# Causal attention with a decaying bias, followed by a GELU feed-forward, on one core: other loads of the first k, chunk 0 by pairs of subtiles, v of batch 2 behind the x tiles

## The chip, the core and the metric

The kernel runs on one core of a Trainium2 chip. The time is the device time of one execution in microseconds (us); the figure to compare is the median over several runs. TensorE does the matrix products, VectorE and ScalarE the element-wise work, GpSimd and SyncE mostly issue DMAs. In the profile they are called PE, DVE, ACT, POOL and SP; PEld is TensorE's loading of weights, and SPq is SyncE's queue of DMA issues.

## The reference

q, k and v have the shape (8 batches, 8 heads, 576 positions, 64), s has (8, 8, 576). The feed-forward has 512 inputs, 2048 hidden units and 512 outputs, all in fp32.

```
scores = scale * np.matmul(q, k.transpose(0, 1, 3, 2))
cum = np.cumsum(np.maximum(s, 0.0), axis=-1)
bias = -(cum[:, :, :, None] - cum[:, :, None, :])
scores = np.where(causal, -1000000000.0, scores + np.minimum(bias, 0.0))
attn = softmax(scores)                       # max subtracted, exp, divided by the sum
x = np.matmul(attn, v), laid out as (8 * 576 tokens, 8 * 64)
out = gelu_exact(x @ w_in) @ w_out
```

## The kernel before, in words

**How the bias is handled.** The bias is a difference of a term of the row and a term of the column. The row's term cancels in the softmax, so `weights` (L217) forms exp(cum) for each position, `scale_v` (L202, on VectorE) multiplies v by it, and `den_col` (L212) puts it into a 65th column of v, which gives the sum. At the end a certificate (`cert_decay` L239, `cert_1` to `cert_4`) proves from the largest q, k (`absmax` L188, VectorE) and v (`square_v` L194, ScalarE) that this shortcut was exact enough; otherwise a slow path runs, which these inputs don't take.

**Loads.** `load_qk` (L85) brings q (i = 0) or k (i = 1) of one batch and one group of four heads in four DMAs of 32 partitions, from GpSimd's queue, which turns fp32 into bf16 on the way. `load_v` (L109) brings v of a batch in five DMAs as fp32, from the queue it is given. `load_w` (L130) brings a quarter of w_in (which = 0) or of w_out (which = 1), again cast by GpSimd's queue. A buffer called rawv (L106) exists twice, so v of batch b + 2 waits until v of batch b has been read.

**Attention of a batch.** `tr_qk` (L180) transposes 32 x 32 blocks of q or k on VectorE. `sc_item` (L329) multiplies k and q for a group g and a half u of the blocks below the diagonal, and takes the exp on ScalarE; `sc_first` (L353) does this for batch 0 and adds the mask on TensorE. `mk_item` (L340) masks the diagonal blocks on VectorE. `av_item` (L403) multiplies with v for a group and a row tile `it` of 128 positions, and divides by the sum on VectorE (L418, L419). When both groups of a row tile are there, `to_xT` (L383) transposes it, by a DMA on SyncE's queue (L388), or on TensorE with a copy by VectorE (L392, L395).

**Feed-forward.** The 4608 tokens are taken in nine chunks of 512, which straddle the batches. `l1_item` (L430) computes 256 hidden units of a chunk on TensorE (L441) and their gelu on ScalarE (L446). `l2_item` (L450) sums over a range of the 16 hidden tiles for given subtiles of 128 tokens (L457), copies each finished subtile out of its output buffer (L465 by ScalarE in chunk 0, L467 by VectorE in the others), and stores it. The output buffers have the tag mlp, and there are two of them.

**Order.** Every engine executes its instructions in the order in which the program lists them; that order is written by hand. In the main loop (L532) chunk c runs layer 1, with late attention items of batch c and the transposes, scaling and squares of batch b = c + 1 between its eight items. Then it runs layer 2 in four subtiles of four slots each (`groups`, L477). After slot i the items in `side[i]` follow, the attention of batch c + 1. Chunk 0 has its own lists (`late` L539 and `side` L578). Exp and gelu are in different tables of ScalarE: `exp_set` (L471) and `gelu_set` (L474) load them. `filler` (L397) issues matmuls on zeros.

On GpSimd's queue the order after the start is: v of batch 0 (two pieces), w_in 0, v (three pieces), w_in 1 to 3, then for each group two quarters of w_out and q and k of batch 1, then v of batch 1, then q and k of batch 2 (L490 to L500, L597). On SyncE's queue v of batch 2 is issued ahead of the fourth subtile of chunk 0 (L591).

Of the kernel before, what the change touches and what calls it, by code (L numbers as in the profile page):

```python
# [19 lines left out]
def kernel(  # L20
# [10 lines left out]
    nc = tc.nc  # L31
    fp32 = mybir.dt.float32
# [52 lines left out]
    def load_qk(b, i, g):  # L85

        if (b, "qk") not in raws:
            raws[b, "qk"] = work.tile([128, 2, HG, S * 2], bf16, tag="rawqk", bufs=2, name="raw_qk")
        src = q if i == 0 else k
        for h in range(4):  # L90
            nc.gpsimd.dma_start(  # L91
                out=raws[b, "qk"][h * 32 : h * 32 + 32, i, g, :].rearrange("p (t c) -> p t c", c=2 * D),
                in_=bass.AP(
                    tensor=src.tensor,
                    offset=src.offset + (b * H + 4 * g + h) * S * D,
                    ap=[[2 * D, 32], [64 * D, SB], [1, 2 * D]],
                ),
            )

    def load_qks(b):  # L100
        for g in range(HG):
            for i in range(2):
                load_qk(b, i, g)
# [5 lines left out]
    def load_v(b, eng, sts=range(ST)):  # L109
        t = raws[b, "v"] if (b, "v") in raws else raw_v(b)  # L110
        for st in sts:
# [7 lines left out]
                ),  # L119
            )  # L120

    s_sw = const.tile([64, S], fp32, name="s_sw")
    nc.sync.dma_start(out=s_sw, in_=s.flatten_outer_dims())
    load_qk(0, 0, 0)
    load_qk(0, 1, 0)

    w_in_r = const.tile([128, KO, dff], bf16, name="w_in_r")
    w_out_r = const.tile([128, FT, KO * 128], bf16, name="w_out_r")
# [19 lines left out]
        channel_multiplier=1,  # L148
    )
    load_qk(0, 0, 1)  # L150
    load_qk(0, 1, 1)
    amx = const.tile([128, B * HG, 2], fp32, name="amx")
    wb = const.tile([128, ST, BH], bf16, name="wb")
    xT = const.tile([128, NP, n_tok], bf16, name="xT")
# [81 lines left out]
    def le(dst, a, thr, op=ALU.is_le):  # L236
        nc.vector.tensor_scalar(dst, a, float(thr), None, op0=op)

    def cert_decay():  # L239

        w64 = work.tile([64, S], fp32, tag="w64", bufs=1, name="w64")
        nc.scalar.activation(w64, cum, func=AF.Exp)
        W = const.tile([64, ST], fp32, name="cW")
        nc.vector.tensor_reduce(
            W[:, 0 : ST - 1], w64[:, 0:512].rearrange("p (s c) -> p s c", c=128), axis=AX, op=ALU.add
        )
        nc.vector.tensor_reduce(W[:, ST - 1 : ST], w64[:, 512:S], axis=AX, op=ALU.add)

        le(goods[:, 0:1], cum[:, 0:1], -MAX_C, ALU.is_ge)
        le(goods[:, 1:2], cum[:, 511:512], 2.0, ALU.is_ge)  # L250
        le(goods[:, 2:3], cum[:, S - 1 : S], MAX_C)
        le(goods[:, 3:4], cum[:, 255:256], -14.0, ALU.is_ge)

        nc.vector.tensor_copy(drop[:, 0:1], W[:, 0:1])
        nc.vector.tensor_tensor(drop[:, 1:2], drop[:, 0:1], W[:, 1:2], op=ALU.add)
        nc.vector.tensor_tensor(drop[:, 2:3], drop[:, 1:2], W[:, 2:3], op=ALU.add)
        le(goods[:, 4:5], drop[:, 1:2], 2.0)
        nc.vector.tensor_tensor(keep[:, 0:1], drop[:, 2:3], W[:, 3:4], op=ALU.add)
        le(goods[:, 5:6], keep[:, 0:1], math.exp(66.0))

        nc.vector.tensor_scalar(keep, W[:, 1:4], EPS, None, op0=MULT)
# [135 lines left out]
    def filler(n):  # L397

        f_ps = ps.tile([128, NB], fp32, tag="mlp", bufs=2, name="f_ps")
        for _ in range(n):  # L400
            nc.tensor.matmul(f_ps, lhsT=zero[:, :128], rhs=zero, start=True, stop=True)  # L401
# [69 lines left out]
    def exp_set():  # L471
        nc.scalar.preload_act_table_set("natural_log_exp_and_others")
# [11 lines left out]


    exp_set()
    filler(16)
    weights()
    filler(5)
    load_v(0, nc.gpsimd, range(2))  # L490
    load_w(0, 0)
    load_v(0, nc.gpsimd, range(2, ST))
    for i in range(1, 4):
        load_w(0, i)
    for g in range(HG):
        load_w(1, 2 * g)
        load_w(1, 2 * g + 1)
        for i in range(2):
            load_qk(1, i, g)
    load_v(1, nc.gpsimd)  # L500
    tr_qk(0, 0, 0)
    masks()
# [3 lines left out]
    den_col(0)  # L506
    tr_qk(0, 0, 1)
    tr_qk(0, 1, 1)
    filler(4)
    for st in range(2):  # L510
        scale_v(0, st)
    sc_first(1, 0)
    av_item(0, 0, 0)
    av_item(0, 0, 1)
    sc_first(1, 1)
# [3 lines left out]
    to_xT(0, 0, True)  # L519
    filler(1)  # L520
    to_xT(0, 1, True)
    for st in range(2, ST):
        scale_v(0, st)
    gelu_set()

    sc, mk, av = sc_item, mk_item, av_item
# [5 lines left out]
    for c in range(NCH):  # L532
        b = c + 1
        if c > 0 and b + 1 < B:
            load_qks(b + 1)
            load_v(b + 1, nc.sync)
        if c == 0:

            late = [  # L539
                [(av, 0, 0, 2)], [(av, 0, 1, 2)], [(av, 0, 0, 3)], [(av, 0, 1, 3), (to_xT, 0, 2, True)],  # L540
                [(av, 0, 0, 4)], [(av, 0, 1, 4), (to_xT, 0, 3, True)], [], [(to_xT, 0, 4, True)],
            ]
            for half in range(2):
                for f2 in range(FT // 2):
                    l1_item(0, f2, half * 256, half * 256 + 256)
                    for f, *a in late[f2] if half == 0 else []:
                        f(*a)
                    if half == 1 and 1 <= f2 <= ST:
                        square_v(0, f2 - 1)
            for g in range(HG):  # L550
                absmax(0, g)
        else:
            for f2 in range(FT // 2):
                l1_item(c, f2)
                for g, it in late_of.get(c, [])[f2 : f2 + 1]:
                    av(c, g, it)
                if b < B and f2 < HG:
                    tr_qk(b, 0, f2)
                    tr_qk(b, 1, f2)
                if b < B and f2 == 2:  # L560
                    den_col(b)
                    for st in range(2):
                        scale_v(b, st)
                if b < B and f2 == 3:
                    for st in range(2, ST):
                        scale_v(b, st)
                if b < B and 4 <= f2 < 4 + HG:
                    absmax(b, f2 - 4)
                if b < B and 1 <= f2 <= ST:
                    square_v(b, f2 - 1)  # L570
        if b < B:
            if c == 0:
                for i in range(2):
                    tr_qk(b, i, 0)
                den_col(b)
            exp_set()
            if c == 0:
                side = [[] for _ in range(16)]  # L578
                side[2] = [(sc, b, 0, 0)]
                side[5] = [(sc, b, 0, 1), (mk, b, 0, 0), (tr_qk, b, 0, 1), (tr_qk, b, 1, 1)]  # L580
                side[7] = [(scale_v, b, 0), (scale_v, b, 1), (mk, b, 0, 1)]
                side[8] = [(sc, b, 1, 0), (av, b, 0, 0), (scale_v, b, 2)]
                side[9] = [(av, b, 0, 1), (scale_v, b, 3)]
                side[10] = [(av, b, 0, 2), (mk, b, 1, 0), (scale_v, b, 4)]
                side[11] = [(sc, b, 1, 1), (av, b, 0, 3), (av, b, 1, 0)]
                side[12] = [(av, b, 1, 1), (mk, b, 1, 1)]
                side[14] = [(av, b, 1, 2, True), (av, b, 1, 3, True)]
                side[15] = [(to_xT, b, 2, True), (to_xT, b, 3, True)]
                for sub in range(4):
                    if sub == 3:  # L590
                        load_v(2, nc.sync)  # L591
                    groups(c, (sub,), side[4 * sub : 4 * sub + 4])
                for st in range(ST):
                    square_v(b, st)
                cert_decay()
                gelu_set()
                load_qks(2)  # L597
                for g in range(HG):
                    absmax(b, g)
            else:  # L600

                side = [[] for _ in range(16)]
                sc_at = (2, 5, 7, 10) if b < 4 else (2, 5, 8, 11)
                for at, (g, u) in zip(sc_at, [(0, 0), (1, 0), (0, 1), (1, 1)]):
                    side[at].append((sc, b, g, u))
                side[sc_at[3]].append((gelu_set,))
                for at, (g, u) in zip((5, 8, 11, 13 if b < 4 else 14), [(0, 0), (1, 0), (0, 1), (1, 1)]):
                    side[at].append((mk, b, g, u))
                for at, (g, it) in zip((6, 7, 9, 10), [(0, 0), (0, 1), (1, 0), (1, 1)]):
                    side[at].append((av, b, g, it))  # L610
                if b < 4:
                    side[12].append((av, b, 0, 2))
                    side[13].append((av, b, 1, 2, True))
                    side[14].append((to_xT, b, 2, True))
                for sub in range(4):
                    groups(c, (sub,), side[4 * sub : 4 * sub + 4])
        else:
            for sub in range(4):
                l2_item(c, (sub,))
                if c == B - 1:  # L620
                    (cert_1, cert_2, cert_3, cert_4)[sub]()
# [150 lines left out]
```

## Time and profile before

| | |
|---|---|
| median of 5 runs | 337.67 us (335.5 to 338.04) |
| profiled execution | 339.84 us |
| its span, first to last instruction | 338.1 us |
| mean granted clock of TensorE | 0.976 |
| PE busy | 315.5 us (93%) |
| DVE, ACT, POOL busy | 190.2, 185.1, 92.1 us |
| layer 1 of chunk 0 | from 24.50 us |
| layer 2 of chunk 0 | from 41.23 us |
| layer 1 of chunk 1 | from 73.72 us |
| layer 1 of chunk 2 | from 110.26 us |
| read from, written to memory | 36.85 MB, 9.44 MB |

The profile is of one execution. Times within it count from its first instruction. A line of the chain of waits or of the timeline has the start, the duration, the engine, the line of the program, the operation and the tiles written and read; in brackets stands how long the engine was idle before, and what ended that. "x4" is the number of instructions put together. A line of the waits view has the engine and line that waited, what it waited for, the total, the number of times and the longest. The clock row gives tenths of the full clock in 40 slices of the span, where 9 stands for nine tenths or more.

### The profile page before, as it was taken

The page shows a single profiled execution, that of the slowest core. Times are in us where ns is not written, and L with a number is a line of the kernel's source. Part 1 is how long each engine was busy: PE and PEld are TensorE (multiplying, and loading weights), DVE is VectorE, ACT ScalarE, POOL GpSimd, SP SyncE. Part 2 cuts the span into 40 slices and gives each one's busy share as a digit, 9 for nine tenths or more (in the row PEclk, how much of TensorE's full clock was granted, in tenths as well). Part 3 has the DMA queues.
Part 4 walks back from the last instruction along what each step waited for, and adds up shares of the span by engine and source line. Part 5 has one row for each costly group of instructions (what it writes and reads, how often), then busy time and mean ns, then how long its engine had stood idle before and what let it go on. Part 6 is the DMA issues. An engine that isn't in the chain of part 4 may idle for free.

```text
span 338.1 us, 6339 instructions
## 1 busy us (share of the span) xinstructions
PE 315.5 (93%) x2554; PEld 157.3 (47%) x2554; DVE 190.2 (56%) x393; ACT 185.1 (55%) x247; POOL 92.1 (27%) x152
## 2 busy tenths in 40 slices
PE   8999969729998999899999999999999999999992
PEld 3358824414444544454455444545454545444440
DVE  7355815777746783679358845965695542150020
ACT  2464855545864586558567755776587464205400
POOL 8962657608490009000910190000000000000000
PEclk9999989967999999999999999999999999999998
DMA  8999999999794709670997198901310221110011
GB/s 90 147 231 202 116 160 237 163 233 168 67 149 109 183 14 137 129 181 17 120 146 186 27 149 138 182 8 64 93 33 8 80 80 31 41 62 32 3 66 67
DMA packets 92373, 36.76 MB, mean 109 GB/s; under 512 B 82992, under 2 KB 87088, under 8 KB 92336
## 3 DMA queue, kind: packets, MB, share of 16 engines
q0 software_dynamic: 43872, 16.00, 39.8%
q1 hardware_dynamic: 48464, 20.28, 23.6%
q8 instruction: 22, 0.36, 0.5%
q14 instruction: 15, 0.12, 0.1%
HBM read 36.85 MB, written 9.44 MB: 137 GB/s over the span
## 4 chain that ended last, share of the span: by engine, by line
PE 75%; DMA 14%; POOL 6%; DVE 2%; issue 1%; ACT 1%; POOLq 0%
PE h_ps L441 34%; PE o_ps L457 32%; DMA w_out_r<-in_moe_w_out_dram 7%; POOL raw_qk L91 5%; PE av L409 4%; PE sc_ps L321 4%; DMA w_in_r<-in_moe_w_in_dram 2%; DMA raw_v<-in_v_dram 2%; POOL raw_v L113 1%; DMA raw_qk<-in_k_dram 1%; DMA xT<-x 1%; DVE P L344 1%; DVE o_sb L467 1%; ACT sq L197 0%; DVE x L419 0%
## 5 line engine op out<-in xcount | busy, mean ns | idle before, releaser
L441 PE MATMUL h_ps<-xT,w_in_r 128*128 128x512 bf16 (+1 forms) x640 | 135.4, 363 | 8.4 <-DMA xT<-x 7.7
L457 PE MATMUL o_ps<-w_out_r,gT 128*128 128x512 bf16 x576 | 136.7, 382 | 2.8 <-DMA w_out_r<-in_moe_w_out_dram 2.8
L446 ACT ACTIVATE gT<-h_ps 128x1024 bf16<-128x1024 f32 (+1 forms) x80 | 75.0, 939 | 76.8 <-PE h_ps L441 76.1
L441 PEld LDWEIGHTS <-w_in_r 128*128 128x128 bf16 x640 | 60.1, 99 | 64.0 <-DMA xT<-x 7.8
L457 PEld LDWEIGHTS <-gT 128*128 128x128 bf16 x576 | 52.3, 98 | 60.7 <-issue 7.0
L336 ACT ACTIVATE P<-sc_ps 128x1024 bf16<-128x1024 f32 x56 | 54.3, 1021 | 37.1 <-PE sc_ps L321 37.1
L91 POOL DMA_DIRECT2D raw_qk<-in_q_dram x64 | 38.7, 621 | 94.0 <-DVE amx L189 89.6
L467 DVE COPY o_sb<-o_ps 128x512 f32<-128x512 f32 x32 | 22.1, 692 | 63.8 <-PE o_ps L457 63.8
L91 POOL DMA_DIRECT2D raw_qk<-in_k_dram x64 | 38.8, 626 | 14.0 <-DMA w_out_r<-in_moe_w_out_dram 7.8
L189 DVE TENSOR_REDUCE amx<-raw_qk 128x2 f32<-128x2304 bf16 x16 | 40.2, 2536 | 0.0
L418 DVE RECIPROCAL rc<-av 128x4 f32<-128x4 f32 (+1 forms) x80 | 14.3, 179 | 42.9 <-PE av L409 42.8
L409 PEld LDWEIGHTS <-P 128*128 128x128 bf16 x576 | 27.4, 98 | 19.7 <-DVE P L344 3.4
L419 DVE TENSOR_TENSOR x<-av,rc 128x256 bf16<-128x256 f32 (+1 forms) x80 | 33.8, 423 | 2.8
L409 PE MATMUL av<-vv,P 128*128 128x65 bf16 x576 | 31.3, 194 | 2.4 <-DVE P L344 2.0
L205 DVE TENSOR_TENSOR vv<-raw_v,wb 128x512 bf16<-128x512 f32 (+1 forms) x40 | 25.9, 690 | 5.6 <-DMA raw_v<-in_v_dram 5.6
L182 DVE STREAM_TRANSPOSE qkT<-raw_qk 128x576 f32<-128x576 f32 x32 | 23.3, 757 | 7.3 <-DMA raw_qk<-in_k_dram 4.3
L344 DVE TENSOR_TENSOR P<-P,tri_bf 128x1024 bf16<-128x1024 bf16 x28 | 19.2, 685 | 11.9 <-ACT P L336 11.9
L197 ACT ACTIVATE sq<-raw_v 128x512 bf16<-128x512 f32 (+1 forms) x40 | 24.8, 622 | 0.0
L321 PE MATMUL sc_ps<-qkT 32*128 32x256 bf16 (+2 forms) x560 | 18.4, 254 | 0.0
L321 PEld LDWEIGHTS <-qkT 32*128 32x128 bf16 x560 | 11.9, 94 | 13.1 <-issue 12.3
L401 PE MATMUL f_ps<-zero 128*128 128x512 bf16 x36 | 11.4, 433 | 1.2 <-DVE zero L140 1.2
L379 ACT ACTIVATE P<-sc_ps 128x1024 bf16<-128x1024 f32 x8 | 8.2, 1024 | 7.0 <-PE sc_ps L374 7.0
(74 smaller groups left out, 97.9 us busy)
## 6 DMA issues: line engine op xcount, KB each, us to landing
out_dram<-o_sb SPq DMA_DIRECT2D x36, 256.0 KB, 2.2
raw_v<-in_v_dram SPq DMA_DIRECT2D x24, 256.0 KB, 4.1
raw_qk<-in_q_dram POOLq DMA_DIRECT2D x64, 72.0 KB, 3.5
raw_qk<-in_k_dram POOLq DMA_DIRECT2D x64, 72.0 KB, 3.8
raw_v<-in_v_dram POOLq DMA_DIRECT2D x8, 256.0 KB, 6.8
w_in_r<-in_moe_w_in_dram POOLq DMA_DIRECT2D x4, 512.0 KB, 11.3
w_out_r<-in_moe_w_out_dram POOLq DMA_DIRECT2D x4, 512.0 KB, 11.9
raw_v<-in_v_dram SPq DMA_DIRECT2D x6, 128.0 KB, 3.9
```

The lines of the kernel that those rows point to most:

```text
L91: nc.gpsimd.dma_start(out=raws[b, "qk"][h * 32 : h * 32 + 32, i, g, :].rearrange("p (t c) -> p t c", c=2 * D), in_=bass.AP(tensor=src.tens ...
L189: nc.vector.tensor_reduce(amx[:, b * HG + g], raws[b, "qk"][:, :, g, :], axis=AX, op=ALU.max, apply_absolute_value=True,)
L197: nc.scalar.activation(sq[:n_st], raws[b, "v"][:n_st, st].rearrange("p h d -> p (h d)"), func=AF.Square, accum_out=sumv[:n_st, b, st : st ...
L205: nc.vector.tensor_tensor(vv[b % 2][:n_st, st, :, 0:D], raws[b, "v"][:n_st, st, :, :], w.unsqueeze(2).to_broadcast([n_st, H, D]), op=MULT,)
L321: nc.tensor.matmul(s_ps[h // 2][:, h % 2, off : off + n], lhsT=qk[r, 1, g, jt * 128 : jt * 128 + 128, e], rhs=qk[r, 0, g, i0 : i0 + n, e], ...
L336: nc.scalar.activation(P[:, 2 * h2 : 2 * h2 + 2, o : o + 512], s_ps[h2], func=AF.Exp, scale=scale)
L409: nc.tensor.matmul(o_ps[:, h, :], lhsT=P[:, h, off : off + 128], rhs=vv[b % 2][:, jt, 4 * g + h, :], start=(i == 0), stop=(i == len(BLK[it ...
L419: nc.vector.tensor_tensor(x_of[b, it][:n, g * 256 : g * 256 + 256].rearrange("p (h d) -> p h d", d=D), o_ps[:n, :, 0:D], rc[:n].unsqueeze( ...
L441: nc.tensor.matmul(h_ps[:, i, :], lhsT=w_in_r[:, ko, ft * 128 : (ft + 1) * 128], rhs=xT[:, ko, c * NB + n0 : c * NB + n1], start=(ko == 0) ...
L446: nc.scalar.activation(gT_of[c][:, f2 * 2 : f2 * 2 + 2, n0:n1], h_ps, func=AF.Gelu)
L457: nc.tensor.matmul(y_of[c, sub], lhsT=gT[:, ft, sub * 128 : (sub + 1) * 128], rhs=w_out_r[:, ft, :], start=(ft == 0), stop=(ft == FT - 1),)
L467: nc.vector.tensor_copy(o_sb, y_of[c, sub])
```

## The change

It has five parts. Line numbers here are those of the kernel before.

1. k of batch 0 is no longer loaded by GpSimd's queue. Its eight DMAs go to ScalarE's queue (group 0) and SyncE's (group 1), as fp32 into a buffer with the tag rawv, and ScalarE casts each group into `raw_qk`. The first cast stands ahead of `weights` on ScalarE, the second behind it.
2. GpSimd's order: w_out's quarters 2 and 3 stand behind q and k of batch 1, group 0, and between q and k of group 1.
3. At the start four fillers between the scores of batch 0's groups go and one of five ahead of them; the last three `scale_v` of batch 0 move between the late items of chunk 0.
4. Layer 2 of chunk 0 runs subtiles 0 and 1 together (eight slots of two hidden tiles each), then 2, then 3; the side items are dealt out anew. v of batch 2 is issued on SyncE's queue behind this.
5. `square_v` leaves layer 1 for layer 2: that of batch 0 goes into layer 2 of chunk 0, that of batches 2 to 7 ahead of the load of the gelu table. That of batch 1 moves from the end of chunk 0 into layer 1 of chunk 1. `cert_decay` is split: its exp runs in layer 2 of chunk 1, the rest in layer 1 of chunk 2.

```diff
+    k0_st = work.tile([128, HG, S * 2], fp32, tag="rawv", bufs=2, name="k0_st")
+    def load_k0(g, eng):
+        for h in range(4):
+            eng.dma_start(
+                out=k0_st[h * 32 : h * 32 + 32, g, :].rearrange("p (t c) -> p t c", c=2 * D),
+                in_=bass.AP(
+                    tensor=k.tensor,
+                    offset=k.offset + (4 * g + h) * S * D,
+                    ap=[[2 * D, 32], [64 * D, SB], [1, 2 * D]],
+                ),
+            )
+    def cast_k0(g):
+        nc.scalar.activation(raws[0, "qk"][:, 1, g, :], k0_st[:, g, :], func=AF.Copy)
...
+    load_k0(0, nc.scalar)
+    load_k0(1, nc.sync)
     load_qk(0, 0, 0)
-    load_qk(0, 1, 0)
...
     load_qk(0, 0, 1)
-    load_qk(0, 1, 1)
...
+    def cert_exp():
+        nc.scalar.activation(w64, cum, func=AF.Exp)
...
     exp_set()
+    cast_k0(0)
     filler(16)
     weights()
-    filler(5)
-    load_v(0, nc.gpsimd, range(2))
+    cast_k0(1)
+    filler(4)
+    load_v(0, nc.gpsimd, (0, 1))
     load_w(0, 0)
-    load_v(0, nc.gpsimd, range(2, ST))
-    for i in range(1, 4):
-        load_w(0, i)
-    for g in range(HG):
-        load_w(1, 2 * g)
-        load_w(1, 2 * g + 1)
-        for i in range(2):
-            load_qk(1, i, g)
+    load_v(0, nc.gpsimd, (2,))
+    load_w(0, 1)
+    load_v(0, nc.gpsimd, (3, 4))
+    load_w(0, 2)
+    load_w(0, 3)
+    load_w(1, 0)
+    load_w(1, 1)
+    for i in range(2):
+        load_qk(1, i, 0)
+    for i in range(2):
+        load_w(1, 2 + i)
+        load_qk(1, i, 1)
     load_v(1, nc.gpsimd)
...
-    filler(4)
+    sc_first(1, 0)
     for st in range(2):
         scale_v(0, st)
-    sc_first(1, 0)
...
-    for st in range(2, ST):
-        scale_v(0, st)
...
-                [(av, 0, 0, 2)], [(av, 0, 1, 2)], [(av, 0, 0, 3)], [(av, 0, 1, 3), (to_xT, 0, 2, True)],
-                [(av, 0, 0, 4)], [(av, 0, 1, 4), (to_xT, 0, 3, True)], [], [(to_xT, 0, 4, True)],
+                [(scale_v, 0, 2), (av, 0, 0, 2)], [(av, 0, 1, 2)],
+                [(scale_v, 0, 3), (av, 0, 0, 3)], [(av, 0, 1, 3), (to_xT, 0, 2, True)],
+                [(scale_v, 0, 4), (av, 0, 0, 4)], [(av, 0, 1, 4), (to_xT, 0, 3, True)],
+                [], [(to_xT, 0, 4, True)],
...
-                    if half == 1 and 1 <= f2 <= ST:
-                        square_v(0, f2 - 1)
...
-                if b < B and 1 <= f2 <= ST:
-                    square_v(b, f2 - 1)
+                if c == 2 and f2 == 7:
+                    cert_decay()
+                if c == 1 and 1 <= f2 <= ST:
+                    square_v(c, f2 - 1)
...
+                for st in range(3):
+                    square_v(0, st)
                 side = [[] for _ in range(16)]
...
+                side[3] = [(sc, b, 0, 0)]
+                side[5] = [(sc, b, 0, 1), (mk, b, 0, 0), (square_v, 0, 3), (square_v, 0, 4)]
+                side[6] = [(tr_qk, b, 0, 1), (tr_qk, b, 1, 1)]
+                side[9] = [(mk, b, 0, 1), (scale_v, b, 0)]
+                side[10] = [(sc, b, 1, 0), (scale_v, b, 1)]
+                side[11] = [(av, b, 0, 0), (scale_v, b, 2)]
+                side[12] = [(av, b, 0, 1), (sc, b, 1, 1), (mk, b, 1, 0), (av, b, 0, 2), (scale_v, b, 3)]
+                side[13] = [(av, b, 1, 0), (av, b, 0, 3), (scale_v, b, 4)]
+                side[14] = [(av, b, 1, 1), (mk, b, 1, 1)]
+                side[15] = [
+                    (av, b, 1, 2, True), (av, b, 1, 3, True), (to_xT, b, 2, True), (to_xT, b, 3, True)
+                ]
+                groups(c, (0, 1), side[:8])
+                groups(c, (2,), side[8:12])
+                groups(c, (3,), side[12:])
                 gelu_set()
                 load_qks(2)
+                load_v(2, nc.sync)
...
+                for st in range(ST):
+                    side[sc_at[3]].append((square_v, b, st))
                 side[sc_at[3]].append((gelu_set,))
...
+                if c == 1:
+                    side[3].append((cert_exp,))
```

More of the change, by code (lines that the diff above doesn't have):

```diff
@@ L237, in le @@
         nc.vector.tensor_scalar(dst, a, float(thr), None, op0=op)
+    w64 = work.tile([64, S], fp32, tag="w64", bufs=1, name="w64")
+    def cert_exp():
+        nc.scalar.activation(w64, cum, func=AF.Exp)
     def cert_decay():
-        w64 = work.tile([64, S], fp32, tag="w64", bufs=1, name="w64")
-        nc.scalar.activation(w64, cum, func=AF.Exp)
         W = const.tile([64, ST], fp32, name="cW")
@@ L577 @@
             if c == 0:
+                for st in range(3):
+                    square_v(0, st)
                 side = [[] for _ in range(16)]
[L579 to L595, printed above, removed]
+                side[3] = [(sc, b, 0, 0)]
[13 more added lines that the diff above has]
+                groups(c, (3,), side[12:])
                 gelu_set()
                 load_qks(2)
+                load_v(2, nc.sync)
                 for g in range(HG):
```

## The prediction

> **What bounds the kernel now.** The page's slices and chain come first.
>
> ```profile
> PEclk9999989967999999999999999999999999999998
> DMA  8999999999794709670997198901310221110011
> PE 75%; DMA 14%; POOL 6%; DVE 2%; issue 1%; ACT 1%; POOLq 0%
> ```
>
> From about 85 us TensorE (PE) at full clock is the chain. Ahead of that DMA and POOL are, the DMA engines are busy, and the clock falls (slices of 8.45 us). So the start-up and chunk 0 are where time can be won. PE's waits up to 74 us, longest first (total, times, longest):
>
> ```profile
> PE h_ps L441 <- DMA xT<-x: 7.7, 1, 7.7
> PE o_ps L457 <- DMA w_out_r<-in_moe_w_out_dram: 2.8, 2, 2.0
> PE f_ps L401 <- DVE zero L140: 1.2, 1, 1.2
> ```
>
> SyncE's queue (SPq) around the first of these:
>
> ```profile
> 62.52 1.31 SPq L388 DMA_TRANSPOSE xT<-x  x1
> 64.01 6.26 SPq L113 DMA_DIRECT2D raw_v<-in_v_dram  x5
> 70.38 1.24 SPq L388 DMA_TRANSPOSE xT<-x  x1
> ```
>
> The x tile of item 1 waits 6.26 us behind the issues of v of batch 2; it lands 3.3 us after its own issue, at 73.67, and layer 1 of chunk 1 starts at 73.72. It starts cold (span, busy and matmuls of PE, of weight loads, clock, DMA, GB/s, for L441 alone):
>
> ```profile
> 73.70:80.30 6.60, 6.33 (x16) 1.99 (x16) 0.55 1.10 209
> 80.50:91.00 10.50, 10.46 (x48) 4.63 (x48) 1.00 1.02 98
> ```
>
> Warm, 16 matmuls take 16 x 10.5/48 = 3.5 us; here 6.6: 3.1 us lost. The start:
>
> ```profile
> 3.81 2.46 POOL L91 DMA_DIRECT2D raw_qk<-in_k_dram  x4
> 8.41 0.78 DVE L182 STREAM_TRANSPOSE qkT<-raw_qk 128x576 f32<-128x576 f32 x1 [0.80 <-DMA raw_qk<-in_k_dram]
> 9.29 2.38 POOL L91 DMA_DIRECT2D raw_qk<-in_k_dram  x4
> ```
>
> Up to 14 us each q or k load costs POOL 0.6 us and lands 2.6 us later: issue sets the pace. From 15 us on, loads land 5 to 15 us after issue: the engines' backlog does.
>
> **What the skill says.** (1) The Trainium skill, "DMA: Bandwidth & Descriptors", section "Issuing engines are not separate DMA queues": DMAs of all queues share the same 16 engines; more queues save only issue time. The trace agrees for after 15 us; before it, issue time is just what is short. (2) Same page, "SWDGE vs HWDGE vs iDMA": a cast during DMA is possible only from GpSimd. So k by hardware queues arrives as fp32 and needs a cast; no run here shows it. (3) "ScalarE: Activation LUTs", "What ACT_TABLE_LOAD costs": 186 ns + 0.833 ns per element. For 1024 that is 1039; the trace has 1021 (L336). (4) "TensorE: Matmul & The Clock Gate", "What's actually happening": the clock halves after an idle window of some 3.4 us and recovers after a busy one. The trace shows 0.55 after the 7.7 us wait. It also shows a fall near 49 us after holes of 0.9 and 2.0 us, so a partly idle window is enough here.
>
> **The change, part by part.**
>
> *k by hardware queues.* POOL loses eight issues: 2.46 + 2.38 = 4.84 us, so q of group 1, v, w_in and w_out are issued that much sooner. ScalarE gets four issues ahead of its table load, SyncE four behind s; a SyncE issue took 0.35 to 0.6 us (s: 0.59). Two casts are added on ScalarE: 1152 elements by (3), 1.15 us each, an estimate. The first stands ahead of the two exps of `weights` and of all score exps, the second behind those of `weights`. When do scores start (9.25 before)? In the backlog q or k loads land 0.43 us apart (37.20 to 40.59, eight). Best: k of group 0 lands at about 5.3, is cast by 6.5, VectorE is free at 7.6 as before, scores at 8.45. Worst: three queues share the engines, s and twelve loads land by 2.2 + 13 x 0.43 = 7.8, cast 8.95, transposed 9.75, scores 9.8. I take 9.0: -0.25 us (ends -0.8 and +0.55).
>
> *Fillers.* `sc_first(1, 0)` follows the scores of group 0 directly: it ran at 15.93, after four fillers and after k of group 1 (transposed at 15.02), while the scores before it ended at 14.73: -1.2 us. Its q and k now land by 9.5 and are transposed by about 11.5. Layer 1 of chunk 0 starts at 24.50 - 1.45 = 23.05.
>
> *Layer 1 of chunk 0* is PE's (16.7 us). Two `scale_v` of 0.69 us now stand on VectorE between the reciprocals and divisions of late items: about +0.3. Squares leave ScalarE; PE wins nothing. Layer 2 starts at 40.1 (41.23 before).
>
> *Supply.* All of q and k landed at 14.1; now at about 9.4 (last q issue 6.85 plus 2.55): the backlog starts 4.7 us sooner. w_out block 2 then lands at 43.9 - 4.7 = 39.2; block 3, now behind four q loads (4 x 0.43), at 47.5 - 4.7 + 1.7 = 44.5. PE needs block 2 at 40.1 + 16 x 0.216 + 0.6 (scores) = 44.2, since each block now serves two subtiles, and block 3 at about 46.9. So the waits of 2.8 us go, and so does the cold clock near 49 us (12 matmuls from 47.55 took 4.00 us, 2.6 when warm).
>
> *Two subtiles at a time: a new wait.* Both output buffers (mlp) are full until the copies L465. ScalarE's order at the seam is: two exps of the second scores, two squares, then the copies. From the scores' end (46.9): 1.94 + 2 x 0.62 + 0.60 = 3.8 us, to 50.7. PE has eight matmuls, 1.7 us, to 48.6. Subtile 2 waits 2.1 us. Nothing covers it.
>
> *Rest of layer 2.* From 50.8: 32 matmuls 6.9, two scores 1.2, the attention items 2.4, transposes 0.8. The last four items now stand in one slot with no matmuls between: mask 0.97, division 0.6 and copies 0.4 of VectorE show, 2.0 in all. PE is ready at 64.1. The x tile of item 1 is issued at about 61 and takes 3.3 to 4.9 us (the two above). I take 64.7. v of batch 2 follows, lands by 70, and VectorE reaches it at about 71 (5.0 us of absmax first).
>
> *Squares and certificate.* Squares of later batches leave layer 1, where ScalarE isn't late, for layer 2, ahead of the gelu table. There ScalarE idles 2.10 us before the first gelu of chunk 3:
>
> ```profile
> 175.03 1.28 ACT L475 ACT_TABLE_LOAD   x1
> 178.41 1.02 ACT L446 ACTIVATE gT<-h_ps 128x1024 bf16<-128x1024 f32 x1 [2.10 <-PE h_ps L441]
> ```
>
> Five squares took 3.06 us (66.06 to 69.12), so this gelu ends 0.96 later, at 180.4; PE needs its buffer for the third item at 180.5. Cost 0, at most 0.3 in each of four chunks. `cert_exp` (0.67) sits in a 1.3 us idle stretch; `cert_decay` (2 us of VectorE) in chunk 2, which has slack. v of batch 3 now waits on SyncE for squares of batch 1, with one x tile and outputs behind it; these are needed 15 us later.
>
> *Sum.* Chunk 1 starts 73.72 - 64.7 = 9.0 us sooner. Of the 3.1 us of cold clock I keep 1.4: PE is under half busy from 61 to 64.7. Gain 9.0 + 1.7 = 10.7 us. The profiled span 338.1 becomes 327.4; that execution took 339.84 in all, 2.2 above the median 337.67. I carry the difference: 337.67 - 10.7 = 327.0.
>
> **Rivals.**
> A, the forecast: 327.0, own range 325 to 329.5. Chance 0.51.
> B, no clock loss and a good start: scores at 8.45, x tile in 3.3 us, clock full: 10.7 + 0.55 + 0.5 + 1.4 = 13.2: 324.5. For it: the holes are 2 us, not 7.7. Against: holes of 2.0 and 0.9 were enough near 49 us. Chance 0.22.
> C, both new holes halve the clock for a window: half of a window of 3.4 us by (4), 1.7, more at the seam and again in chunk 1: 330.4. For it: the same fall. Chance 0.17.
> D, slower: k's arrival. Each us by which k of group 0 lands after about 7 delays the cast, and behind it, in ScalarE's order, everything. Landing at about 17.7 eats the whole gain; at 20 the time is 339.5. For it: hardware loads of v landed only 0.4 to 1.6 us apart under load, with three queues active. Against: four loads at that worst pace still land by 9. Chance 0.05.
> E, the x tile wait only changes its cause: the tile lands at 73 because loads of q and k for batch 2 are ahead. For it: w_out took 15.2 us to land in a backlog. Against: that was on the software queue; on SyncE the tile took 4.9 at worst. Time 335 to 338. Chance 0.05, no-change 0.03 of it.
>
> About 0.5% is what a measurement can tell from no change. Faster 0.92 (A, B, C, part of E), same 0.03, slower 0.05. The range, 321.5 to 332, spans A, B and C with 2 us for the unknown ends.
>
> **What would show it.** The wait of L441 on the x tile falls from 7.7 to below 2; the two x tiles stand on SPq ahead of v; L457's wait on w_out is gone, and a wait of about 2 us on the copy L465 stands at the seam; layer 2 of chunk 0 starts near 40, layer 1 of chunk 1 near 65; chunks 2 to 8 keep their lengths. Wrong if: scores start after 10, w_out still ends waits, or layer 1 of chunk 1 starts later than 67.

## The result

| | before | changed |
|---|---|---|
| median | 337.71 us (79 runs) | 339.3 us (42 runs) |
| ratio to the kernel before | | 1.0059, 95% interval 1.0046 to 1.0072 |
| profiled execution, its span | 339.84, 338.1 us | 338.81, 337.0 us |
| first scores | 9.25 us | 11.71 us |
| layer 1 of chunk 0 | 24.50 us | 33.64 us |
| layer 2 of chunk 0 | 41.23 us | 51.10 us |
| layer 1 of chunk 1 | 73.72 us | 75.12 us |
| its end less the start of chunk 1 | 264.4 us | 261.9 us |

The change makes the kernel 0.6% slower; 327.0 us, 3% faster, was forecast. The profiled execution of before lies 2.2 us above its median, that of the changed kernel 0.5 below; so the two spans stand the other way round than the medians. For the experiments, medians and ratios leave out executions more than 1.5% above the fastest of the same kernel; where one of these bears on the argument, it is named.

The page of the changed kernel, with its clock, its DMA share and its chain:

```profile
PEclk9655999999999999999999999999999999999999
DMA  9999999439999819570988197701310221110011
...
PE 83%; DVE 7%; DMA 3%; POOL 2%; issue 2%; ACT 1%; DVEq 0%; POOLq 0%; ACTq 0%
```

The chain lies on the DMA engines for 3% of the span instead of 14%, and on VectorE for 7% instead of 2%. The clock no longer falls near 49 us and from 69 to 80 us, as it did before, but it is halved from about 12 to 32 us, where it was full. TensorE's longest waits up to 90 us (total, times, longest):

```profile
PE sc_ps L385 <- DVE qkT L199: 3.6, 1, 3.6
PE o_ps L476 <- ACT o_sb L484: 1.9, 1, 1.9
PE av L428 <- DVE vv L222: 1.4, 3, 0.5
```

The 7.7 us on the x tile and the 2.8 us on w_out are gone. In their place stand a wait of the first scores on the transposed q and k, the wait at the seam between subtiles 1 and 2, and three small ones on scaled v. SyncE's queue shows why the x tile is on time: both transposes go out ahead of v.

```profile
70.22 2.89 SPq L407 DMA_TRANSPOSE xT<-x  x2
73.21 0.54 SPq L488 DMA_DIRECT2D out_dram<-o_sb  x1
73.98 2.15 SPq L113 DMA_DIRECT2D raw_v<-in_v_dram  x3
```

Layer 1 of chunk 1 then runs warm from its first matmul (L460 alone; columns as in the forecast):

```profile
75.10:81.70 6.60, 6.42 (x29) 2.65 (x29) 1.00 0.81 182
```

29 matmuls in the 6.6 us in which 16 fitted before. So what the change was to win around chunk 1 was won. It was lost at the start. The chain of waits, and the timeline of ScalarE and VectorE there:

```profile
3.22 6.25 DMA raw_qk<-in_q_dram
9.59 0.78 DVE qkT L199
```

```profile
8.32 1.16 ACT L137 ACTIVATE raw_qk<-k_st 128x1152 bf16<-128x1152 f32 x1 [4.34 <-DMA k_st<-in_k_dram]
9.59 0.78 DVE L199 STREAM_TRANSPOSE qkT<-raw_qk 128x576 f32<-128x576 f32 x1 [3.06 <-DMA raw_qk<-in_q_dram]
10.29 0.48 DVE L193 TENSOR_SCALAR neg_bf<-uptri 128x128 bf16<-128x128 f32 x1
10.88 0.77 DVE L199 STREAM_TRANSPOSE qkT<-raw_qk 128x576 f32<-128x576 f32 x1
```

k of group 0 is late (its cast can start only at 8.32), but q is later: its last load of group 0 is issued at 3.22 as before, and takes 6.25 us to land instead of 2.6. The masks (L193 to L195), which VectorE used to do while it waited for k, now stand in the way between q and k. And TensorE has nothing to do meanwhile. By stages (span, busy and instructions of PE, PEld, DVE, ACT, POOL, clock, DMA, GB/s):

```profile
8.10:11.70 3.60, 0.03 (x1) 0.00 (x0) 2.12 (x7) 2.59 (x4) 3.60 (x6) 1.00 1.44 249
11.70:31.40 19.70, 19.70 (x151) 7.30 (x152) 3.83 (x10) 7.94 (x8) 8.58 (x13) 0.50 1.24 207
31.40:51.10 19.70, 18.23 (x205) 15.55 (x203) 14.68 (x29) 10.49 (x17) 12.61 (x19) 0.98 1.07 161
```

The same stage in the kernel before:

```profile
9.20:22.40 13.20, 13.15 (x157) 6.07 (x158) 4.33 (x10) 7.57 (x8) 10.90 (x16) 1.00 1.10 191
```

The fillers end at 8.1; 3.6 us of nothing follow; then the whole score phase runs at clock 0.50, and 151 matmuls take 19.7 us where 157 took 13.2.

### The profile page after: what moved, and what is told of

Same layout as the page of the kernel before. It is cut to its first block, busy times and chain, and to the rows that moved or that the text cites. A ratio compares the mean times of both kernels' runs of the same rounds, so it can differ in the third digit from the quotient of the medians.

```text
span 337.0 us, 6343 instructions
## 1 busy us (share of the span) xinstructions
PE 318.3 (94%) x2549; PEld 158.0 (47%) x2549; DVE 189.4 (56%) x393; ACT 187.6 (56%) x249; POOL 87.8 (26%) x144
## 4 chain that ended last, share of the span: by engine, by line
PE 83%; DVE 7%; DMA 3%; POOL 2%; issue 2%; ACT 1%; DVEq 0%; POOLq 0%; ACTq 0%
PE h_ps L460 35%; PE o_ps L476 32%; PE av L428 5%; PE sc_ps L340 4%; PE sc_ps L385 3%; DMA raw_qk<-in_q_dram 3%; POOL raw_qk L91 2%; PE sc_ps L393 2%; DVE x L438 2%; PE f_ps L420 1%; DVE P L363 1%; DVE vv L222 1%; DVE amx L206 1%; ACT sq L214 1%; ACT P L355 1%
## 5 line engine op out<-in xcount | busy, mean ns | idle before, releaser
L476 PE MATMUL o_ps<-w_out_r,gT 128*128 128x512 bf16 x576 | 135.3, 379 | 1.9 <-ACT o_sb L484 1.9
L460 PE MATMUL h_ps<-xT,w_in_r 128*128 128x512 bf16 (+1 forms) x640 | 132.6, 358 | 1.4 <-DVE xT L414 1.0
L460 PEld LDWEIGHTS <-w_in_r 128*128 128x128 bf16 x640 | 59.9, 98 | 55.1 <-issue 2.1
L428 PEld LDWEIGHTS <-P 128*128 128x128 bf16 x576 | 28.2, 99 | 20.9 <-DVE P L363 3.9
L91 POOL DMA_DIRECT2D raw_qk<-in_k_dram x56 | 34.1, 644 | 11.8 <-DMA w_out_r<-in_moe_w_out_dram 6.7
L428 PE MATMUL av<-vv,P 128*128 128x65 bf16 x576 | 32.2, 196 | 3.7 <-DVE P L363 2.3
L420 PE MATMUL f_ps<-zero 128*128 128x512 bf16 x31 | 12.8, 527 | 1.2 <-DVE zero L158 1.2
```

What stands on the lines that cost most here:

```text
L91: nc.gpsimd.dma_start(out=raws[b, "qk"][h * 32 : h * 32 + 32, i, g, :].rearrange("p (t c) -> p t c", c=2 * D), in_=bass.AP(tensor=src.tens ...
L428: nc.tensor.matmul(o_ps[:, h, :], lhsT=P[:, h, off : off + 128], rhs=vv[b % 2][:, jt, 4 * g + h, :], start=(i == 0), stop=(i == len(BLK[it ...
L460: nc.tensor.matmul(h_ps[:, i, :], lhsT=w_in_r[:, ko, ft * 128 : (ft + 1) * 128], rhs=xT[:, ko, c * NB + n0 : c * NB + n1], start=(ko == 0) ...
L476: nc.tensor.matmul(y_of[c, sub], lhsT=gT[:, ft, sub * 128 : (sub + 1) * 128], rhs=w_out_r[:, ft, :], start=(ft == 0), stop=(ft == FT - 1),)
```

## The experiments

The theory after the first look: the start alone turns the gain into a loss, and more through the clock than through the lateness. The rival: the rest of the change is worth nothing. "Changed" below is the changed kernel; "the hole" is the time in which TensorE has nothing to do ahead of the first scores.

**1. Changed, with the start of before** (the helpers `load_k0` and `cast_k0` go too).

```diff
-    load_k0(0, nc.scalar)
-    load_k0(1, nc.sync)
     load_qk(0, 0, 0)
+    load_qk(0, 1, 0)
...
     load_qk(0, 0, 1)
+    load_qk(0, 1, 1)
...
-    cast_k0(0)
     filler(16)
     weights()
-    cast_k0(1)
-    filler(4)
+    filler(5)
...
-    sc_first(1, 0)
+    filler(4)
     for st in range(2):
         scale_v(0, st)
+    sc_first(1, 0)
```

> The changed kernel with the start of the kernel before (k of batch 0 by GpSimd's queue, five and four fillers). Theory (the start alone loses the gain: scores from 11.7 us on a halved clock, layer 1 of chunk 0 at 33.6 instead of 24.5; the rest of the change pays about as forecast): scores start near 9.3, layer 1 of chunk 0 near 24.5, layer 1 of chunk 1 near 66; 329 to 331 us. Rival (the pairs of subtiles, the moved v and the squares pay nothing; the start costs little in the end): 337 or more.

Measured: 329.67 us (13 of 20 executions), ratio 0.9767 (0.9745 to 0.9789). Scores from 9.56, layer 1 of chunk 0 from 25.00, of chunk 1 from 66.93. The rival falls: all but the start is worth 2.3%. But seven executions took 337.2 to 338.4 us, nearly 8 us more. Their mean clock is 0.946 to 0.965, like the changed kernel's (0.954 to 0.969 in all its executions), where the thirteen have 0.988 to 0.998. So this start, with a hole of 0.6 us in the profile, probably loses the clock in a third of its executions; no profile of one was kept, so it isn't shown.

**2. Before, with only the start of the changed kernel** (the reverse of the diff above).

> The kernel before with only the start of the changed one (k of batch 0 by two hardware queues as fp32 with casts, and its fillers). Theory (the start is a loss by itself): scores at 11.7, clock halved until about 32, layer 1 of chunk 0 near 33.6; some of it is absorbed later because the loads are there by then; 341 to 345 us. Rival (the start costs little): within 1 us of the kernel before.

Measured: 339.87 us, ratio 1.0055 (1.0031 to 1.0079). Layer 1 of chunk 0 starts at 34.60, 10 us late, the clock is 0.50 from 11.9 to 34.6; but layer 1 of chunk 1 starts at 74.96, only 1.2 us late. The theory had the sign right and the size too high: 341 to 345. Of the 10 us, 8.9 are absorbed. The wait on w_out (2.8) is gone, and that on the x tile falls from 7.7 to 5.2 us: loads had come in meanwhile. That is 5.3 us; the halved clock behind the wait on w_out is gone too, and the rest wasn't traced. The same start costs 9.6 us in the changed kernel (339.3 against 329.7), which no longer has those waits.

**3. Changed, with the hole filled.**

```diff
     cast_k0(1)
-    filler(4)
+    filler(22)
```

> The changed kernel with 22 fillers instead of 4 behind the weights' transposes, so that TensorE is busy from 8 to about 11.7 us until the first scores. Theory (the clock does most of the harm, not the lateness): scores still start near 11.7 to 12, but at full clock; layer 1 of chunk 0 near 26; 331 to 333 us. Rival (lateness of q and k itself costs the time): gain under 2 us, 337.5 or more.

Measured: 331.76 us, ratio 0.9836 (0.9776 to 0.9896). Nothing about q, k or their casts is changed, and the scores come even later, at 12.39. The two rows are the former hole and the score phase up to 24.5 us:

```profile
8.10:12.30 4.20, 4.20 (x21) 1.76 (x18) 2.55 (x7) 2.59 (x4) 3.92 (x5) 1.00 1.44 247
12.40:24.50 12.10, 12.10 (x148) 5.57 (x148) 3.21 (x8) 7.39 (x8) 6.87 (x11) 1.00 1.20 228
```

That is 148 matmuls in 12.1 us. From the first scores to layer 1 it takes 26.77 - 12.39 = 14.4 us, against 33.64 - 11.71 = 21.9: 7.5 us, which is the distance of the medians (339.3 - 331.8). This is shown: the clock takes 7.5 us. The lateness of q and k is worth less: experiment 1, whose scores start 2.8 us earlier, is 2.1 us faster (329.7 against 331.8).

**4. Before, with v of batch 2 behind the x tiles.**

```diff
-                    if sub == 3:
-                        load_v(2, nc.sync)
...
                 load_qks(2)
+                load_v(2, nc.sync)
```

> The kernel before with only the issue of v of batch 2 moved behind the x tiles. Theory (the 7.7 us wait and the 3.1 us of halved clock were caused by that order): layer 1 of chunk 1 starts near 67, warm; 328 to 330 us. Rival (the x tile then waits for other loads in the engines' backlog): 334 or more.

Measured: 331.97 us, ratio 0.985 (0.9786 to 0.9913), halfway between the two expectations. Layer 1 of chunk 1 starts at 66.53 instead of 73.72. The x tile still ends a wait of 2.9 us, and the clock is still halved for 3.4 us from 66.8 on. So this move brings 1.5% of the 2.3% of experiment 1: the tile takes 5.0 us to land (issued at 61.36, landed at 66.39) among q and k loads, as the rival said, but by a smaller amount.

**5. Changed, with only group 0 of k on a hardware queue.**

```diff
     load_k0(0, nc.scalar)
-    load_k0(1, nc.sync)
...
     load_qk(0, 0, 1)
+    load_qk(0, 1, 1)
...
-    cast_k0(1)
     filler(4)
```

> The changed kernel, but only group 0 of k comes by ScalarE's queue (cast by ScalarE); group 1 goes back to GpSimd's queue behind q of group 1. Theory (q of group 0 landed at 9.5 instead of 5.8 because eight fp32 loads of k shared the engines with it): with four of them q lands near 6.5, scores start near 8.6, TensorE is idle for less than 1 us, the clock stays full; layer 1 of chunk 0 near 23.5; 327 to 330 us. Rival (fp32 loads by hardware queues and the cast are slow in themselves): scores after 10.5 and a halved clock again, 337 or more.

Measured: 328.64 us, ratio 0.9725 (0.9683 to 0.9768). q of group 0 lands at 7.46, between the 5.80 of before and the 9.46 of the change: the fp32 loads of k do delay it, by 0.4 to 0.5 us for each. Scores start at 9.49, not 8.6; that part of the expectation failed, since VectorE again has q, masks and k in a row from 7.59. The hole is 1.6 us. One execution of five, the profiled one, took 336.2 us, 7.6 more, and shows why:

```profile
7.90:9.50 1.60, 0.01 (x2) 0.02 (x3) 1.60 (x6) 0.43 (x3) 1.60 (x4) 1.00 1.31 123
9.50:31.20 21.70, 21.23 (x163) 8.55 (x164) 6.19 (x16) 9.47 (x9) 13.53 (x19) 0.53 1.16 201
```

In this execution the clock was halved behind the hole, up to 31 us; in the other four it evidently wasn't (328.4 to 328.9 us, mean clock 0.995 or more against 0.965). With a hole of 1.6 us it is a matter of chance.

**6. The same with six fillers, and two mends.** The scalings of v go back ahead of layer 1, and the two squares go behind the copies at the seam. (Of the list of late items one row of three is shown.)

```diff
-    filler(4)
+    filler(6)
...
     to_xT(0, 1, True)
+    for st in range(2, ST):
+        scale_v(0, st)
     gelu_set()
...
-                [(scale_v, 0, 2), (av, 0, 0, 2)], [(av, 0, 1, 2)],
+                [(av, 0, 0, 2)], [(av, 0, 1, 2)],
...
-                side[5] = [(sc, b, 0, 1), (mk, b, 0, 0), (square_v, 0, 3), (square_v, 0, 4)]
+                side[5] = [(sc, b, 0, 1), (mk, b, 0, 0)]
+                side[8] = [(square_v, 0, 3), (square_v, 0, 4)]
```

> The kernel of the run with one group of k by ScalarE's queue, with six fillers behind the weights, the last three scalings of v of batch 0 back ahead of layer 1, and the last two squares of batch 0 moved from ahead of the copies at the seam to behind them. Theory: the waits on scaled v (1.4 us) go, the wait at the seam falls from 1.9 to about 0.7 us; 2 us below the run without these mends: 325.5 to 328. Rival (other engines are late at the same places): within 0.7 us of it.

Measured: 327.11 us, ratio 0.9704 (0.9659 to 0.9749), 1.5 us below experiment 5; fillers and mends are together in it. The waits on scaled v fall from 1.4 to 0.4 us, that at the seam from 1.9 to 0.7:

```profile
PE h_ps L460 <- DMA xT<-x: 1.2, 1, 1.2
PE o_ps L476 <- ACT o_sb L484: 0.7, 1, 0.7
```

**7. Experiment 1 with the two mends**, that is with all of k by GpSimd's queue.

> The changed kernel with the start of the kernel before (all of k by GpSimd's queue) and the same two mends: scalings of v ahead of layer 1, squares behind the seam's copies. Theory: 2 us below the same without mends (331.2): 329; and 1 to 2 us above the run that has k of group 0 by ScalarE's queue. Rival (the early k is worth nothing even without the hole): equal to that run.

Measured: 329.79 us, ratio 0.974 (0.9687 to 0.9794), no faster than experiment 1 (329.67) and 2.7 us above experiment 6. The profile, of an execution of 331.69 us, says where the mends went: the waits at the seam and on scaled v fall to 0.6 us each, but the x tile's grows from 0.9 to 2.3 us, and the clock is halved for 6.8 us from 63.9 on. In the profile of 6 this doesn't happen. But the executions of 7 range from 327.2 to 332.6 us, and the fastest, with a mean clock of 0.997, is as fast as 6; two of the six executions of 6 took 329.2 and 330.2 us, with 0.988 and 0.985. So the two kernels differ mainly in how often the clock is lost; with the clock kept, the mends seem to pay (327.2 to 329.8 us with a mean clock of at least 0.993, against 329.3 to 330.3 in experiment 1) and the early k little. These are few executions: it is a hint, not shown.

**8. Changed, with a dense stretch after the hole.**

```diff
     tr_qk(0, 1, 1)
+    filler(16)
     sc_first(1, 0)
```

> The changed kernel with 16 fillers between the scores of group 0 and those of group 1, after the hole. Theory (the score phase keeps whatever clock it finds, and only a dense stretch of matmuls brings it back): the clock is back within 7 us of the first of these fillers, near 27, the scores of group 1 run at full clock, layer 1 of chunk 0 near 35; 340 us. Rival (the clock comes back only after a fixed time, near 32): layer 1 of chunk 0 near 38 to 40, 344 us.

Measured: 339.95 us, ratio 1.0068 (1.0043 to 1.0094). The rows are scores of group 0, the fillers, scores of group 1 up to layer 1:

```profile
12.30:21.30 9.00, 9.00 (x64) 2.97 (x65) 2.58 (x5) 3.09 (x4) 5.27 (x8) 0.50 1.14 216
21.30:25.00 3.70, 3.70 (x10) 1.31 (x9) 0.00 (x0) 1.00 (x1) 1.50 (x3) 0.53 1.24 206
25.00:35.20 10.20, 9.66 (x108) 4.55 (x106) 3.05 (x11) 5.38 (x5) 4.06 (x7) 1.00 1.28 165
```

The clock is back 3.5 us after the first of these fillers, at 24.8, instead of at 32.3. The expectation held, and the rival falls: it isn't a fixed time. The score phase doesn't bring the clock back, a dense stretch does.

**9 and 10. What pairs of subtiles are worth, and how sure six fillers are.** Experiment 9 is before with v behind the x tiles (4) and the start of 6. Experiment 10 is 6 with `filler(10)`.

> The kernel before with v of batch 2 behind the x tiles and with the start of the mended kernel (k of group 0 by ScalarE's queue, six fillers, no fillers between the groups); subtiles one at a time, squares and the order of weights as before. Theory (pairs, weights' order and moved squares together are worth 1 to 3 us, because waits on w_out of some 2 us give way to 0.7 us at the seam): 328.5 to 330. Rival (they are worth nothing): 327 as the mended kernel.

> The mended kernel with ten fillers behind the weights instead of six. Theory (a hole of 1 us ahead of the scores still halves the clock in some executions): median the same within 0.5 us, no execution above 330. Rival (fillers delay the scores): 0.9 us slower, four fillers of 0.22 us.

Measured: 330.62 us, ratio 0.9784 (0.9746 to 0.9822), and 326.9 us, ratio 0.9678 (0.9648 to 0.9708), executions from 326.4 to 327.4. Experiment 9 meets neither expectation. In its profile the clock is halved for 17 us behind a hole of 0.8 us, so 9 tells nothing of pairs alone. The kernel before has a hole of the same length at the same place, and its clock stayed full (the first line is of before, the second of 9):

```profile
PE sc_ps L366 <- DVE qkT L182: 0.8, 1, 0.8
PE sc_ps L383 <- DVE qkT L199: 0.8, 1, 0.8
```

In the profile of 10 scores start at 10.3, 0.8 later than in 6, on a TensorE that isn't idle ahead of them, and the median is that of 6 within 0.2 us; both expectations of the theory held. This is the steadiest version, and it beats both kernels.

**11. Experiment 9 with ten fillers.**

> The run without pairs (subtiles one at a time, squares and order of weights as before), with ten fillers behind the weights instead of six, so that no hole is left ahead of the scores. Theory (the run without pairs was partly the halved clock, and pairs, weights' order and squares are worth about 1 to 2 us): 328 to 329.5, waits on w_out of some 2 us instead of the 0.7 us at the seam. Rival 1 (pairs are worth nothing, the whole distance was the clock): 327. Rival 2 (they are worth it all): 330.5.

Measured: 329.6 us, ratio 0.9751 (0.9719 to 0.9783); no halved clock at the start. Against 10 the pairs, the order of w_out, the moved squares and the split certificate together are worth 0.7%, about 2.7 us; a little more than expected, and not for the reason given:

```profile
PE h_ps L458 <- DMA xT<-x: 3.8, 1, 3.8
PE o_ps L474 <- DMA w_out_r<-in_moe_w_out_dram: 0.2, 1, 0.2
```

The wait on w_out is 0.2 us only. It is the x tile that is late without them, by 3.8 us, and the clock is halved for 3.4 us at the start of chunk 1. Which of the four parts brings the gain wasn't separated.

## Why the prediction was wrong, point by point

**The step that failed: "I take 9.0: -0.25 us (ends -0.8 and +0.55)."** Two things were wrong in it, and a term was missing.

- *The landing of q.* The worst case had all early loads landed at 2.2 + 13 x 0.43 = 7.8 us. The first of these thirteen landed at 3.40 (2.6 in the sum) and the others about 0.5 apart, the last one, of q's group 0, at 9.46. So the sum began 0.8 us too early, and its pace cost another 0.9. And q, whose issues GpSimd spaces out, came last among three queues, even behind k of group 1; behind the landings the forecast followed k alone.
- *VectorE's order.* The masks were in no term of the sum, as if done while k is awaited, which was so before. With q last they stand between q and k: 1.3 us from the start of q's transpose to that of k's, 2.1 to the scores.
- *The clock.* It had no term at all. The forecast counted how late the scores would be and not what TensorE does until then. The fillers end at 8.1 us, and TensorE did nothing for 3.6 us. The text even had the evidence, "a partly idle window is enough here", and used it for the seam and chunk 1 only. Experiment 3 measures what this term is: 7.5 us, the largest part of the miss. The rest of the 10.6 us by which layer 1 of chunk 0 came later than forecast (33.64 for 23.05) is the 2.7 us of later scores and 0.4 elsewhere.

The median missed by 12.3 us (339.3 for 327.0), of which 9.6 are in the profiled span (337.0 for 327.4). The other 2.7 are a second step that failed: "I carry the difference". The profiled execution of before was 2.2 us above its median, that of the changed kernel 0.5 below, so this distance was no property of the kernel.

Rival D had the right place, k's arrival and what is behind it, and the wrong price: "each us ... delays", with a break-even at 17.7 us. In fact the cast began at 8.32, and a hole of 3.6 us was enough. (By its own rate its time at 20 us is 340.0, not 339.5.)

**What was right.**

- *v behind the x tiles:* the wait of 7.7 us is gone, and chunk 1 starts warm. I kept 1.4 us for the clock there; none was lost, and from the start of chunk 1 to the end the run is 2.5 us shorter for a forecast of 1.7. The tile landed 2.3 us after its issue, less than the 3.3 to 4.9 taken; the last of the q and k loads had landed at 61.6, 10 us before its issue.
- *Supply:* all early q and k landed at 11.1 us, 3.0 sooner than before, not 4.7, as the last took 4.4 us to land and not 2.55; block 2 of w_out at 40.3 and block 3 at 44.6 (39.2 and 44.5 forecast). No wait on w_out is left.
- *Seam:* 1.9 us for a forecast of 2.1, with the cause as told: ScalarE does two exps and two squares ahead of the copies.

```profile
57.97 1.94 ACT L355 ACTIVATE P<-sc_ps 128x1024 bf16<-128x1024 f32 x2 [0.71 <-PE sc_ps L340]
59.80 0.63 ACT L214 ACTIVATE sq<-raw_v 128x512 bf16<-128x512 f32 x1
60.41 0.62 ACT L214 ACTIVATE sq<-raw_v 64x512 bf16<-64x512 f32 x1
61.02 1.06 ACT L484 ACTIVATE o_sb<-o_ps 128x512 f32<-128x512 f32 x2
```

- *Layer 2 of chunk 0:* 24.0 us, which is what the forecast had for TensorE's own work; it added 0.6 for the x tile, which in fact was there in time.
- *Cast:* 1.16 us for 1.15. The formula of the Trainium skill ("ScalarE: Activation LUTs", "What ACT_TABLE_LOAD costs") holds here.
- *Squares in layer 2:* the chunk that the forecast calls 3 is chunk 4, by the starts of layer 1. There the first gelu starts at 177.88, 2.9 us after layer 1 (2.0 before); layer 1 takes 15.34 us, 15.26 before. Chunks 2 to 8 together take 228.3 us, 227.8 before. "Cost 0, at most 0.3 in each of four chunks" holds.
- *Scalings between late items:* three waits, 1.4 us in all; layer 1 of chunk 0 takes 17.46 us, 0.7 more than before, where 0.3 was forecast. The place was right, the size too small.

Put right, the sum is: forecast start of chunk 1 at 64.7, plus 10.6 from the start, plus 0.4 in layer 1, less 0.6 in layer 2: 75.1, as measured. With no hole (experiment 10) chunk 1 starts at 63.7.

One rule of the Trainium skill is too narrow for this case. "TensorE: Matmul & The Clock Gate", "What's actually happening", has the clock fall after an idle window of some 3.4 us; here holes of 3.6 to 4.2 us did it in each of the three profiles taken of such a start, but 1.6 and 0.8 us did it too in executions of experiments 5 and 9. The measurement decides: a hole well below a window can be enough. It need not be: a hole of 0.8 us left the clock full in the kernel before.

What stays open: when exactly a hole costs the clock, whether six fillers are as safe as ten (six leave no idle time in the profile, but two of six executions were 2 to 3 us slower), and how much of the difference between 6 and 7 is due to the earlier loads.

## What to carry to other kernels

When a transfer moves to another queue, ask who was using the DMA engines at that moment: it overtakes somebody, here the q that was needed first. And for any step that delays TensorE's first real work, count what keeps TensorE busy until then: a hole costs its own length once, but if the clock is lost with it, that was paid for over the whole phase behind it here. Where fillers are in place for that, their number belongs to the arrival time they were tuned to, and has to be changed with it.

## What the runs showed of the hardware that was not expected

The clock has a memory. The score phase (matmuls of 32 rows, some of 128 x 128, one filler for each pair of heads) kept a full clock full for 13 us (kernel before) and a halved one halved for 20 us (changed kernel), though the trace shows TensorE busy all the time in both. Sixteen fillers in a row brought it back within 3.5 us.

The length of a hole alone doesn't decide. Ahead of the scores 0.8 us cost the clock in experiment 9 and not in the kernel before; 1.9 us of waiting on w_out cost it in experiment 4 (halved from 46.3 to 49.7 us), and 1.9 us at the seam of the changed kernel didn't. In the clock record of all the profiles, each stretch of halved clock that ends within the run lasts a whole number of steps of 3.41 us: one step in experiment 4, four in 8, six in the changed kernel. If the clock is set once per step, it matters how much of a step a hole fills, and with what the rest is filled. That would explain the chance in experiments 1 and 5; it wasn't tested.

Early loads of 144 KB (read) from three queues at once landed about 0.5 us apart, nearly as fast as such loads in a backlog (0.43). From issue to landing the first took 2.7 us and the later ones up to 6.3, against 2.6 when, but for the load of s, GpSimd's queue alone was active and its issues, 0.6 us apart, set the pace.
